# Low parts of eight weight pieces made by matrix products with plus and minus the identity instead of a VectorE subtraction

## Chip, core and metric

The kernel runs on one NeuronCore of one Trainium2 chip. The metric is the device time of one execution, in microseconds (us), lower is better. The core has TensorE (PE; its weight loads are listed apart as PEld), VectorE (DVE), ScalarE (ACT), GpSimd (POOL) and SyncE (SP, which here only issues transfers). Every engine has a queue of its own; they meet by semaphores.

## What is computed

A pooled attention, then a two-layer network with a leaky ReLU, then a mixture of eight experts with one expert for each token. Cut to what matters here:

```python
k_p = k.reshape(B, H, S // 8, 8, D).mean(axis=3)      # v_p likewise
attn = softmax(q @ k_p.T / sqrt(D))
x = attn @ v_p                                        # 4608 tokens x 512
h = x @ moe_w_in                                      # float64 weights, 512 x 2048
x = maximum(0.01 * h, h) @ moe_w_out                  # float64 weights, 2048 x 512
...
out[mask] = gate_w[mask, None] * (relu(x[mask] @ w1[e]) @ w2[e])
```

`moe_w_in` and `moe_w_out` come as 64-bit floating point numbers; all others as 32-bit.

## The kernel before

**Number format.** A product of the large stages is not done in fp32. Each operand is split into a high part (the value rounded to the type fp32r, in which TensorE streams a column in one pass) and a low part (value minus high part), and a product is the sum of three: high by high, high by low, low by high. So every weight tile holds both parts side by side. The low part is made with `sub`, a `tensor_tensor` subtraction (line 132, the line of the helper); the high part with `act_copy`, a copy on ACT (line 129).

**The dense network** runs over blocks of 256 tokens. A slot of the program is one pair (block b, piece f): `g1` (line 498) multiplies the block by the 128 columns of piece f of `moe_w_in` in twelve products, of which the third is the first to read a low part of the weights; ACT and DVE apply the leaky ReLU; two slots later `g2` (line 526) multiplies the result by piece f of `moe_w_out` in six products of 512 columns. There are sixteen pieces of either matrix. Slots 0 to 3 are pieces 0 to 3 of block 0; from slot 4 on, blocks 0 and 1 take turns.

**The weight pieces** are converted during the first slots. `w_load64` fetches a raw piece, 64-bit numbers, into one of seven raw tiles. `w_conv1` (lines 463 to 474) turns it into fp32 in place: ACT takes the absolute value of the top halfword (463) and prepares from it a word `e` (464) for the exponent; then DVE builds the fp32 word with four integer operations of 512 columns (465, 468, 471, 474), the first and last of which read `e`. The result lies in every second 32-bit word of the raw tile. `w_conv2` then writes the high part by ACT and the low part by DVE into the weight tile (tile `w00` and so on for `moe_w_in`, kind 0; `w10` and so on for `moe_w_out`, kind 1).

**The order of the work** is the order of the code: the program is emitted under a manual schedule, and each engine's queue follows it. A slot emits `g1`, the low part of an earlier activation (`g_lo`), the slot's hooks (attention steps for tokens still to come), the `g2` of two slots before, then `conv`, then the high part of the activation. In slots 0 to 3 `conv` does, for both kinds, first `w_conv2` of piece f+1 and then `w_conv1` of piece f+2. From slot 5 on it does one kind in a slot.

**The hooks of slots 0 to 3** are the attention steps of the third and fourth token tile: `att_a` and `att_b` of tile 2 in slot 0 and of tile 3 in slot 1 (transposes, then two groups of scores, which DVE reduces and subtracts from PSUM: lines 384 and 132), the softmax on ACT and DVE (390 to 399), `att_c` of tile 2 in slot 2 and of tile 3 in slot 3 (transposes, of which ACT takes a high and DVE a low part). In slot 4 `att_av` makes the activations of block 1. All of them take their PSUM bank with `pt("att")`, which hands out two banks in turn, `a0` and `a1`; a new user waits until the last user's readers are done.

Of the kernel before, what the change touches and what calls it, by code (L numbers as in the profile page):

```python
# [9 lines left out]
F32R = mybir.dt.float32r  # L10
# [11 lines left out]
def kernel(  # L22
# [12 lines left out]
    nc = tc.nc  # L35
    P = 128
# [3 lines left out]
    LAG = 4  # L40
# [8 lines left out]
    KD = DM // P  # L49
# [34 lines left out]
    def win(f):  # L84
        return wtile(0, f).rearrange("p (k h n) -> p k h n", k=KD, h=2)

    def wout(f):
        return wtile(1, f).rearrange("p (h n) -> p h n", h=2)
# [7 lines left out]
    ident = pool.tile([P, P], F32, name="ident")  # L96
# [15 lines left out]
    def sb(shape, dt, tag, bufs=1):  # L112
        return pool.tile(shape, dt, name=tag, tag=tag, bufs=bufs)
# [4 lines left out]
    def bank(tag):  # L118
        return psum.tile([P, 512], F32, name=tag, tag=tag)

    def pt(kind):
        turn[kind] += 1
        return bank(banks[kind][turn[kind] % len(banks[kind])])

    def f32(ap):
        return ap.bitcast(F32)

    def act_copy(o, i, scale=1.0):
        nc.scalar.activation(o, i, AF.Copy, scale=scale)  # L129

    def sub(eng, o, a, b):
        eng.tensor_tensor(out=o, in0=a, in1=b, op=ALU.subtract)  # L132
# [344 lines left out]
    def w_conv2(kind, f):  # L477
        w = f32(w_mid.pop((kind, f)))
        if kind == 0:
            w = w.rearrange("p (a n) -> p a n", a=KD)  # L480
            d = win(f)
            dh, dl = d[:, :, 0], d[:, :, 1]
        else:
            dh, dl = wout(f)[:, 0], wout(f)[:, 1]
        act_copy(dh, w)
        sub(nc.vector, dl, w, f32(dh))

    w_raw, w_mid, w_cnt = {}, {}, [0]

# [616 lines left out]
    with tc.manual_schedule():  # L1106
        stack = ExitStack()
        start = stack.enter_context(tc.tile_pool(name="start", bufs=1))
# [51 lines left out]
        att_c(1)  # L1160
        kv_use(0, 6)
        w_conv2(0, 0)
        w_conv1(1, 0)
        att_av(0)
        w_conv2(1, 0)
        kvn_load(0, k, 1)
        w_load64()
# [19 lines left out]
        def conv(s, b, f):  # L1187
            f += LAG * b
            kinds = (b,) if s > LAG and f < NF else (0, 1) if b == 0 else ()
            for kind in kinds:  # L1190
                if (kind, f + 1) in w_mid:
                    w_conv2(kind, f + 1)
                    if w_todo:
                        w_load64()
            for kind in kinds:
                if (kind, f + 2) in w_raw:
                    w_conv1(kind, f + 2)
# [171 lines left out]
```

## Time and profile before

| | |
|---|---|
| median of 3 runs | 1557.83 us (1556.98 to 1558.25) |
| the profiled execution | 1558.05 us, span 1556.0 us |
| granted TensorE clock, mean | 0.975 |
| PE matmul busy | 1472.8 us (95%) |
| PE weight load busy | 1317.6 us (85%) |
| DVE busy | 939.4 us (60%) |
| ACT busy | 626.8 us (40%) |
| POOL busy | 327.3 us (21%) |

The profile is of one execution. Times in it count from the start of the span. A granted clock of 1.00 is 2.4 GHz, of 0.50 1.2 GHz; a value between them in a window means that the clock changed inside it. A row of the timeline gives start, duration, engine, line, operation, output <- inputs, shapes and count, and in brackets the idle time before it and what ended it. Rows of one operation overlap a little at their ends, so the distance from start to start is what an operation costs its engine. An fp32 product appears as two MATMUL instructions, an fp32r product as one. Shares of busy time are averages over stages with different limits. In the trace, slot 0 starts at 35.5 us, and `g1` of slots 1 to 4 end near 49, 59, 69 and 76 us.

### The profile page before, as it was taken

The page shows a single profiled execution, that of the slowest core. Times are in us where ns is not written, and L with a number is a line of the kernel's source. Part 1 is how long each engine was busy: PE and PEld are TensorE (multiplying, and loading weights), DVE is VectorE, ACT ScalarE, POOL GpSimd, SP SyncE. Part 2 cuts the span into 40 slices and gives each one's busy share as a digit, 9 for nine tenths or more (in the row PEclk, how much of TensorE's full clock was granted, in tenths as well). Part 3 has the DMA queues.
Part 4 walks back from the last instruction along what each step waited for, and adds up shares of the span by engine and source line. Part 5 has one row for each costly group of instructions (what it writes and reads, how often), then busy time and mean ns, then how long its engine had stood idle before and what let it go on. Part 6 is the DMA issues. An engine that isn't in the chain of part 4 may idle for free. (4 is left out here: it accounts for less than half of the span.)

```text
span 1556.0 us, 25769 instructions
## 1 busy us (share of the span) xinstructions
PE 1472.8 (95%) x9272; PEld 1317.6 (85%) x9272; DVE 939.4 (60%) x2468; ACT 626.8 (40%) x1442; POOL 327.3 (21%) x294
## 2 busy tenths in 40 slices
PE   3698989999999999999999999999799999999998
PEld 3586879999898888899989989988699999998887
DVE  6998658879778878877877977664122121211111
ACT  4676434544444454444444444322122222222222
POOL 4000012232232233222222332121212111111111
PEclk8699999999999999999999999999899999999999
DMA  9443135555544545535645644143511117566160
GB/s 216 148 132 100 63 99 190 167 188 169 169 167 166 182 149 185 184 140 171 197 153 157 203 149 163 48 178 122 245 41 55 35 48 300 211 257 259 41 250 24
DMA packets 121386, 238.06 MB, mean 153 GB/s; under 512 B 56845, under 2 KB 65041, under 8 KB 117544
## 3 DMA queue, kind: packets, MB, share of 16 engines
q1 hardware_dynamic: 90312, 139.81, 28.7%
q10 hardware_dynamic: 23328, 76.56, 13.0%
q0 software_dynamic: 7616, 20.01, 3.8%
q8 instruction: 75, 1.23, 0.3%
q14 instruction: 55, 0.45, 0.1%
HBM read 317.78 MB, written 87.38 MB: 260 GB/s over the span
## 5 line engine op out<-in xcount | busy, mean ns | idle before, releaser
L526 PE MATMUL y<-w,ghl 128*128 128x512 f32 x1728 | 466.3, 406 | 2.8 <-DVE ghl L132 2.5
L526 PEld LDWEIGHTS y<-w,ghl 128*128 128x128 f32 x1728 | 310.1, 192 | 61.7 <-DVE ghl L132 6.3
L132 POOL TENSOR_TENSOR ps<-ps 128x512 f32<-128x512 f32 x128 | 181.6, 1419 | 482.2 <-ACT ps L129 361.8
L498 PEld LDWEIGHTS h<-x_t,w 128*128 128x128 f32 x1776 | 239.6, 195 | 39.8 <-DVE w L132 16.9
L498 PE MATMUL h<-x_t,w 128*128 128x256 f32 x1776 | 246.4, 288 | 24.0 <-DVE w L132 15.3
L546 DVE CUSTOM_DVE_ANT_0 junk<-y,wg 128x512 bf16<-128x512 f32 x256 | 200.3, 783 | 1.9
L498 PEld LDWEIGHTS y<-x_t,w 128*128 128x128 f32 x1488 | 193.2, 189 | 9.6
L498 PE MATMUL y<-x_t,w 128*128 128x256 f32 x1488 | 196.1, 282 | 0.0
L935 PE MATMUL y<-w,ghl 128*128 128x512 f32 x672 | 176.5, 401 | 0.9 <-DVE ghl L923 0.9
L935 PEld LDWEIGHTS y<-w,ghl 128*128 128x128 f32 x672 | 120.4, 190 | 22.4 <-DVE ghl L923 1.3
L129 ACT ACTIVATE g<-h 128x256 f32<-128x256 f32 x164 | 63.0, 384 | 145.9 <-PE h L498 132.8
L991 POOL DMA_INDIRECT out_dram<-kv,sidx x40 | 40.1, 1003 | 382.5 <-ACT kv L990 199.3
L923 DVE SCALAR_TENSOR_TENSOR ghl<-h,ghl 128x256 fp32r<-128x256 f32 x56 | 23.8, 425 | 135.9 <-ACT ghl L922 135.9
L506 DVE TENSOR_TENSOR h<-g,h 128x256 f32<-128x256 f32 x132 | 56.0, 424 | 77.7 <-ACT g L129 77.2
L132 DVE TENSOR_TENSOR at_t<-a,at_t 128x512 fp32r<-128x512 f32 x62 | 42.7, 688 | 87.6 <-ACT at_t L129 87.2
L129 ACT ACTIVATE ghl<-h 128x256 fp32r<-128x256 f32 x132 | 50.7, 384 | 92.9 <-PE y L526 42.8
L129 ACT ACTIVATE ps<-ps 128x512 fp32r<-128x512 f32 x128 | 80.5, 629 | 17.8 <-DMA ps<-in_moe_w_dram 8.7
L129 ACT ACTIVATE ghl<-y 128x256 fp32r<-128x256 f32 x124 | 47.3, 382 | 95.2 <-DVE y L506 50.5
L132 DVE TENSOR_TENSOR x_t<-a,x_t 128x512 fp32r<-128x512 f32 x60 | 41.1, 688 | 51.7 <-ACT x_t L129 51.7
L129 ACT ACTIVATE g<-y 128x256 f32<-128x256 f32 x124 | 47.4, 382 | 60.9 <-PE y L498 53.4
L295 DVE TENSOR_TENSOR kv<-kv 72x512 f32<-72x512 f32 (+8 forms) x126 | 68.0, 540 | 3.2
L613 POOL DMA_INDIRECT lst<-ent,six x36 | 37.8, 1051 | 150.4 <-DVE six L612 115.1
(291 smaller groups left out, 2157.2 us busy)
## 6 DMA issues: line engine op xcount, KB each, us to landing
w<-wsp SPq DMA_DIRECT2D x108, 2048.0 KB
wsp<-ps ACTq DMA_DIRECT2D x128, 512.0 KB
ps<-in_moe_w_dram SPq DMA_DIRECT2D x128, 256.0 KB
y_d<-y ACTq DMA_DIRECT2D x18, 512.0 KB
q<-in_q_dram SPq DMA_DIRECT2D x28, 256.0 KB
kv<-in_k_dram SPq DMA_DIRECT2D x24, 288.0 KB
kv<-in_v_dram SPq DMA_DIRECT2D x24, 256.0 KB
ps<-in_moe_w_in_dram SPq DMA_DIRECT2D x8, 512.0 KB
```

Source lines behind the costliest of these rows:

```text
L129: nc.scalar.activation(o, i, AF.Copy, scale=scale)
L132: eng.tensor_tensor(out=o, in0=a, in1=b, op=ALU.subtract)
L295: eng.tensor_tensor(out=o, in0=t[:, :, 0:w], in1=t[:, :, w:2 * w], op=ALU.add)
L498: nc.tensor.matmul(p[:, 0:BLK], win(f)[:, kk, l], xv[:, kk, r], start=(n == 0), stop=(n == 3 * KD - 1))
L506: nc.vector.tensor_tensor(out=g, in0=t, in1=h, op=ALU.max)
L526: nc.tensor.matmul(y_ps[b, i], hl[:, l, i * P:i * P + P], wout(f)[:, r], start=(f == 0 and l + r == 0), stop=(last and l == 1),)
L546: nc.vector.tensor_tensor_reduce(out=jk, in0=y_sb[b][:, i], in1=wg_t[0][:, e], scale=1.0, scalar=0.0, op0=ALU.mult, op1=ALU.add, accum_out ...
L613: nc.gpsimd.indirect_dma_start(out=lst, out_offset=bass.IndirectOffsetOnAxis(ap=ix[:, 0:1], axis=0), in_=ent[:, i, :], in_offset=None, bou ...
L923: nc.vector.scalar_tensor_tensor(out=hl[:, 1], in0=b, scalar=0.0, in1=f32(hl[:, 0]), op0=ALU.max, op1=ALU.subtract)
L935: nc.tensor.matmul(o_ps[2 * p + i], hl[:, l, i * P:i * P + P], w[:, r], start=(f == 0 and l + r == 0), stop=(f == 7 and l == 1),)
L991: nc.gpsimd.indirect_dma_start(out=out, out_offset=bass.IndirectOffsetOnAxis(ap=sidx[:, t:t + 1], axis=0), in_=o, in_offset=None, bounds_c ...
```

## The change

For pieces 1 to 4 of both kinds (eight pieces, converted in slots 0 to 3) the low part is no longer a subtraction on DVE. TensorE multiplies the fp32 piece by the identity (an fp32 product of 512 columns) and adds to it, in the same PSUM bank, the high part multiplied by minus the identity (an fp32r product of 512 columns); ACT copies the sum from PSUM into the weight tile. The bank comes from `pt("att")`. Minus the identity is made once, by ACT, in the buffer named `q`, which the load of the fifth token tile takes over in slot 4.

```diff
         act_copy(dh, w)
-        sub(nc.vector, dl, w, f32(dh))
+        if 1 <= f <= LAG:
+            if not minus:
+                minus.append(sb([P, P], F32R, "q"))
+                act_copy(minus[0], ident, -1.0)
+            p = pt("att")
+            pv = p.rearrange("p (a n) -> p a n", a=KD) if kind == 0 else p
+            nc.tensor.matmul(pv, ident, w, start=True, stop=False)
+            nc.tensor.matmul(pv, minus[0], dh, start=False, stop=True)
+            act_copy(dl, pv)
+        else:
+            sub(nc.vector, dl, w, f32(dh))
+
+    minus = []
```

The lines of the changed kernel behind this place are higher by 12 (`g1` is at 510 there, `g2` at 538); the two new products are at 492 and 493.

In ACT's queue, slot 1 before (a0 and a1 are the PSUM banks, w00 and w10 the weight tiles, r64 and kv raw tiles, e0 and e1 the words that `w_conv1` prepares):

```order
L390 ACTIVATE pr_385<-pr_385 128x576
L129 ACTIVATE w02_118<-a0_441 128x512
L129 ACTIVATE w00_301<-r64_114 128x4x128
L129 ACTIVATE w10_332<-kv_115 128x512
L463 ACTIVATE junk_109<-kv_116 128x512
L464 ACTIVATE e0_107<-junk_109,ebias_105 128x512
L463 ACTIVATE junk_109<-ps_110 128x512
L464 ACTIVATE e1_108<-junk_109,ebias_105 128x512
```

and the same place with the change:

```order
L390 ACTIVATE pr_385<-pr_385 128x576
L129 ACTIVATE w02_118<-a0_449 128x512
L129 ACTIVATE w00_301<-r64_114 128x4x128
L129 ACTIVATE w00_301<-a1_466 128x4x128
L129 ACTIVATE w10_332<-kv_115 128x512
L129 ACTIVATE w10_332<-a0_472 128x512
L463 ACTIVATE junk_109<-kv_116 128x512
L464 ACTIVATE e0_107<-junk_109,ebias_105 128x512
L463 ACTIVATE junk_109<-ps_110 128x512
L464 ACTIVATE e1_108<-junk_109,ebias_105 128x512
```

Two copies out of PSUM stand between the high parts and the operations of lines 463 and 464.

In PE's queue, slot 1 with the change, from the slot's `g1` to the next one:

```order
L510 MATMUL h0_425<-x_t_67,w00_301 128x256 x12
L359 MATMUL a0_449<-ident_76,w12_117 128x128 x4
L378 MATMUL a1_455<-kT0_70,w02_118 128x144 x2
L378 MATMUL a0_460<-kT0_70,w02_118 128x144 x2
L492 MATMUL a1_466<-r64_114,ident_76 128x512
L493 MATMUL a1_466<-w00_301,q_398 128x512
L492 MATMUL a0_472<-kv_115,ident_76 128x512
L493 MATMUL a0_472<-w10_332,q_398 128x512
L510 MATMUL h1_491<-x_t_67,w00_301 128x256 x12
```

The four rows of lines 492 and 493 are new, between the scores of `att_b` and the next `g1`; they use the banks a1 and a0 that the two groups of scores used just before.

## Rows read from the trace of the kernel before

**Rows 1.** Windows: us, busy of PE, PEld, DVE, ACT, POOL, then clock, DMA

```profile
41.00:83.00 42.00, 26.23 (x124) 22.79 (x124) 40.60 (x80) 26.81 (x48) 0.00 (x0) 0.72 0.47 146
83.00:175.00 92.00, 81.90 (x472) 68.23 (x471) 84.00 (x164) 58.62 (x121) 0.69 (x3) 0.93 0.30 92
```

**Rows 2.** Waits, 36 to 90 us: us in total, times, longest

```profile
PE h L498 <- DVE w L132: 13.0, 4, 3.9
...
DVE e L465 <- ACT e L464: 0.3, 1, 0.3
```

**Rows 3.** Timeline of DVE, slot 1

```profile
54.92 0.46 DVE L132 TENSOR_TENSOR w<-a,w 128x288 f32<-128x288 f32 x1
...
55.78 0.46 DVE L132 TENSOR_TENSOR w<-a,w 128x288 f32<-128x288 f32 x1
56.15 0.68 DVE L132 TENSOR_TENSOR w<-r,w 128x512 fp32r<-128x512 f32 x1
56.75 0.68 DVE L132 TENSOR_TENSOR w<-kv,w 128x512 fp32r<-128x512 f32 x1
57.35 0.69 DVE L465 SCALAR_TENSOR_TENSOR e<-kv,e 128x512 uint32<-128x512 uint32 x1
...
59.87 0.68 DVE L465 SCALAR_TENSOR_TENSOR e<-ps,e 128x512 uint32<-128x512 uint32 x1
...
62.40 0.41 DVE L506 TENSOR_TENSOR g<-g,h 128x256 f32<-128x256 f32 x1
```

**Rows 4.** Timeline of PE: scores, `g2` at either clock, fp32 products of 512 columns

```profile
50.35 2.29 PE L378 MATMUL a<-kT,w 128*128 128x144 f32 x8 [0.69 <-ACT w L129]
52.26 0.80 PE L498 MATMUL h<-x_t,w 128*128 128x256 f32 x2
...
60.32 2.63 PE L526 MATMUL y<-w,ghl 128*128 128x512 f32 x6
62.84 0.51 PE L498 MATMUL h<-x_t,w 128*128 128x256 f32 x2
...
91.84 1.53 PE L526 MATMUL y<-w,ghl 128*128 128x512 f32 x6
...
116.62 3.65 PE L267 MATMUL a<-w,band 128*64 128x512 f32 x8
```

**Rows 5.** Timeline of ACT, slots 0 and 1

```profile
43.64 0.66 ACT L129 ACTIVATE w<-y 128x512 fp32r<-128x512 f32 x1 [1.82 <-DVE y L474]
44.20 0.64 ACT L463 ACTIVATE junk<-r 128x512 bf16<-128x512 bf16 x1
44.88 0.72 ACT L464 ACTIVATE e<-junk,ebias 128x512 uint32<-128x512 uint16 x1
...
49.70 0.60 ACT L129 ACTIVATE w<-a 128x512 f32<-128x512 f32 x1
50.19 0.68 ACT L129 ACTIVATE w<-r 128x512 fp32r<-128x512 f32 x1
```

**Rows 6.** Timeline of DVE, attention and subtractions of slots 2 and 3

```profile
63.06 0.69 DVE L132 TENSOR_TENSOR at_t<-a,at_t 128x512 fp32r<-128x512 f32 x1
...
66.20 0.68 DVE L132 TENSOR_TENSOR w<-kv,w 128x512 fp32r<-128x512 f32 x1
...
73.11 0.68 DVE L132 TENSOR_TENSOR at_t<-a,at_t 128x512 fp32r<-128x512 f32 x1
...
74.26 1.29 DVE L132 TENSOR_TENSOR w<-ps,w 128x512 fp32r<-128x512 f32 x2
```

**Rows 7.** Windows of one microsecond; the clock is third from the end

```profile
52.00:53.00 1.00, 1.00 (x5) 0.77 (x4) 1.00 (x3) 1.00 (x2) 0.00 (x0) 0.50 0.00 0
62.00:63.00 1.00, 1.00 (x4) 0.57 (x4) 1.00 (x3) 1.00 (x3) 0.00 (x0) 0.76 0.00 0
65.00:66.00 1.00, 0.00 (x0) 0.00 (x0) 0.92 (x3) 0.97 (x3) 0.00 (x0) 0.94 0.00 0
```

**Rows 8.** Waits of PE over the whole span

```profile
PE a L900 <- DMA ps<-y_d,gidx: 9.1, 2, 8.8
```

## The prediction

> **What bounds the kernel now.** I began with the page, whose slices show VectorE (DVE) nearly full and TensorE's clock low early in the span, and cut that stage out. Over 41 to 83 us, where the slots of the change lie, DVE is busy 40.60 of 42.00 us and TensorE (PE) 26.23 [rows 1]. The waits say who holds whom: PE waits 13.0 us, four times, for DVE's write of a weight tile, while DVE waits 0.3 us for ScalarE's (ACT) sign-and-exponent word `e` [rows 2]. So DVE sets the pace, and the four waits are where PE needs the low part of the next piece.
>
> The timeline of DVE gives its order in a slot [rows 3]: at 54.92 and 55.78 the two groups of scores of `att_b` are read out of PSUM, at 56.15 and 56.75 come the two subtractions that the change removes, at 57.35 and 59.87 the repair of the two next raw pieces begins, and at 62.40 the activation of the next `g1`. A subtraction holds DVE for 0.60 us, though its own row says 0.68, since the next starts before its end. A piece's repair holds it 2.52 us (57.35 to 59.87).
>
> Later the delay has nothing to vanish into: from 83 to 175 us DVE is busy 84.00 of 92 us and PE 81.90 [rows 1]. I take what the stage gains or loses to pass to the end one for one.
>
> **The change part by part.** *Removed:* eight subtractions, 8 x 0.60 = 4.80 us of DVE time in a stretch with no free DVE time. By themselves they would give -4.80 us.
>
> *Added on PE:* eight fp32 products of 512 columns and eight fp32r ones. No row before shows the first kind at the low clock. At the full clock four of 512 columns (eight instructions, at 116.62) take 3.65 us, so about 0.90 us each; at the low clock four of 144 columns (eight instructions) take 50.35 to 52.26, or 3.32 ns per column, so 1.70 us for 512 (an estimate from these rows). An fp32r product of 512 columns takes 0.42 us at the low clock (six in 60.32 to 62.84) and about 0.25 us at the full one (six in 1.53) [rows 4]. A pair is thus 2.12 us or 1.15 us.
>
> *Added on ACT:* eight copies out of PSUM of 0.60 us, and one small copy that makes minus the identity, which falls in idle time and which I cost at nothing. ACT has room in total. What counts is where the copies stand. In program order a slot gives ACT: high part, low part out of PSUM, for either piece, and only then the two operations that prepare `e` for the next piece's repair. Before, those two followed the high parts at once. ACT doesn't let an operation that is ready pass one that waits: at 43.64 a copy starts after 1.82 us of waiting for DVE, and the absolute value behind it, whose data come by a transfer and not from DVE, starts at 44.20, after it [rows 5]. So a wait is added on ACT, and queued behind it is the word for which DVE must wait.
>
> *The chain that replaces the subtractions.* The first product needs a PSUM bank of the pair that the slot's attention step has just used, so it starts when DVE has read that bank. From there, at the low clock: both pairs of products 4.24, hand-over 0.05, low part of the second piece 0.60, absolute value 0.68 (44.20 to 44.88), `e` 0.72, hand-over 0.05: 6.34 us until DVE may begin the next repair. At the full clock the second piece's high part is late instead, as it stands on ACT behind the first low part: first pair 1.15, hand-over 0.05, low part 0.49 (49.70 to 50.19), high part 0.68, hand-over 0.05, second fp32r product 0.25, hand-over 0.05, then 0.60 + 0.68 + 0.72 + 0.05 as above: 4.77 us [rows 4, 5].
>
> DVE covers part of it with what it still has to do after freeing the bank:
> - slot 1: the first group's subtraction starts at 54.92 and lasts 0.46, so the bank is free at 55.38 and the product may start at 55.43; DVE has nothing left from 56.15 on. Cover 0.72 us [rows 3]. Slot 0 has the same operations; I take the same.
> - slot 2: bank free at 63.06 + 0.69, softmax work until 66.20. Cover 2.40 us [rows 6].
> - slot 3: bank free at 73.11 + 0.68, DVE free at 74.26. Cover 0.42 us [rows 6].
>
> *Which clock.* TensorE's granted clock is 0.50 (1.2 GHz) at 52 to 53 us though PE is busy all of that microsecond, 0.76 at 62 to 63 after PE has worked for some six microseconds, and 0.94 at 65 to 66, falling, with PE idle there [rows 7]. In slots 1 to 3 PE will again stand idle for several microseconds ahead of the first product, as DVE first does 5.04 us of repair, so I take the low clock for their products, and the full one for slot 0, which follows the dense stretch of the prologue. New DVE waits: 4.77 - 0.72 = 4.05; 6.34 - 0.72 = 5.62; 6.34 - 2.40 = 3.94; 6.34 - 0.42 = 5.92. Sum 19.53, less the 4.80 removed: **+14.7 us**. All four at the full clock: 4.05 + 4.05 + 2.37 + 4.35 = 14.82, so +10.0. All at the low one: 21.10, so +16.3.
>
> The Trainium skill weighs in against my choice: TensorE: Matmul & The Clock Gate, section "What's actually happening", says that activity releases the throttle, and this change adds activity. By that rule alone the sum would be the +10.0; the trace's busy microsecond at 0.50 does not bear it out so early in a burst.
>
> *Edits at no cost.* A raw tile is now free for its reload when the product has read it; these reloads fill tiles used slots later. The load of `q` for the fifth token tile shares its buffer with minus the identity and waits in SP's queue for slot 3's last product; it is read a dozen slots later. If that cover were short, the next transposes of `q` would wait.
>
> *A price no row shows.* The fp32 product streams a word out of every eight bytes; all PE rows here stream adjacent words. ACT reads the same eight-byte step in 0.68 us where a copy out of PSUM takes 0.60 [rows 5], so I take no extra; the other end, half speed, adds 2 x 1.70 per slot, 13.6 us in all. A gain is excluded, as a wider step carries no less. The Trainium skill, SBUF — State Buffer, in its note on cachelines under "The DMA port swizzle", has fp32 reads free up to a step of four elements, so by it no extra; no run here shows that yet.
>
> **The rivals.**
> - *Faster: DVE's relief passes through.* If ACT had `e` ready before DVE is done with attention, the stage would shrink by 8 x 0.60, to 1558.05 - 4.80 = 1553.3 us. For it: DVE is the full engine. It decides at the point where the chain is shorter than the cover (0.42 to 2.40 us); the absolute value and `e` alone take 1.40 us, more than the cover in three of four slots. Chance 0.04.
> - *The full clock in all four slots:* +10.0, 1568.1 us. For it: more PE work per slot. Against: the idle time ahead of each burst. Chance 0.17.
> - *Products at half speed for the eight-byte step:* +14.7 + 13.6 = +28.3, 1586.4 us. Chance 0.07.
> - *The loss is swallowed later,* about 1558 us: it takes a point tied to something other than this chain. The one long PE wait for a transfer, 8.8 us of 9.1, is for rows gathered after the routing [rows 8], which is itself at the end of the chain. Chance 0.03.
> - Forecast (low clock in most slots, +11 to +18): 0.66. The last 0.03 is for losses of another kind.
>
> **How the numbers follow.** The profiled execution took 1558.05 us with a span of 1556.0, and the median of the runs is 0.22 lower. 1558.05 + 14.7 = 1572.8 us. The range 1566 to 1580 holds the forecast, the all-full case at 1568.1 with 2 us of margin, the all-low case at 1574.4, and a third to a half of the half-speed penalty. Out of it stay the full half-speed case, the relief and the swallowed loss, together 0.14 and a little. A measurement of this kernel tells some 0.2% (3 us) from no change. Slower: 0.66 + 0.17 + 0.07 + 0.03 = 0.93; faster 0.04; within 0.2% 0.03.
>
> **What would show it.** In the changed profile DVE should have four waits of 4 to 6 us, all ended by ACT's `e`, where it had 0.3 us; PE's four waits for a weight tile from DVE should be gone, replaced by waits of the first identity product for DVE's reading of the bank. The end of slot 3 should lie about 15 us later, and the stretches after it should be shifted copies. The fp32 products should take about 1.7 us at a clock of 0.50 and 0.9 at 1.00. I am wrong if DVE runs through these slots without idle time, if `e` is written ahead of the low parts, or if the stages behind the slots take back the shift.

## The result and the profile after

| | before | with the change |
|---|---|---|
| median | 1557.4 us (1555.7 to 1558.25, 4 runs) | 1573.8 us (1571.46 to 1578.23, 4 runs) |
| span of the profiled execution | 1556.0 us | 1570.2 us |

The ratio is 1.011 (95% interval 1.0084 to 1.0136): slower, by 16.4 us in the medians and by 14.2 us between the two profiled executions. The forecast was 1572.8.

The page of the changed kernel, busy time of each engine:

```profile
PE 1483.9 (95%) x9296; PEld 1321.2 (84%) x9296; DVE 933.8 (59%) x2460; ACT 630.1 (40%) x1451; POOL 327.4 (21%) x294
```

The totals moved in the directions that the change says: DVE 5.6 us less (the eight rows of 0.68 that are gone make 5.4), PE 11 more, ACT 3.3 more. None of them tells that the kernel got slower. The waits between 36 and 106 us do (columns: us in total, times, longest us):

```profile
ACT w L129 <- PE a L493: 26.3, 8, 7.6
DVE e L465 <- ACT e L464: 21.9, 5, 6.2
...
PE a L492 <- DVE at_t L132: 9.8, 2, 5.0
PE a L492 <- issue: 7.3, 2, 4.4
```

The 13.0 us in which PE waited for DVE's low parts [rows 2] are gone; DVE's 0.3 us of waiting for `e` has become 21.9, and PE waits ahead of the new products. In slots 2 and 3 the profile names DVE's reading of the attention's bank as what ended PE's wait. In slots 0 and 1 it names nothing ("issue"), but there too the first product starts when DVE has just read the bank, 0.10 and 0.09 us after the end of the subtraction (44.31 + 0.46 and 59.62 + 0.46):

```profile
44.31 0.46 DVE L132 TENSOR_TENSOR pr<-a,st 128x288 f32<-128x288 f32 x1
44.87 2.04 PE L492 MATMUL a<-ps,ident 128*128 128x512 f32 x2 [2.93 <-issue]
...
59.62 0.46 DVE L132 TENSOR_TENSOR w<-a,w 128x288 f32<-128x288 f32 x1
60.17 2.04 PE L492 MATMUL a<-r,ident 128*128 128x512 f32 x2 [4.35 <-issue]
```

A circle has closed: PE waits for DVE, ACT for PE, DVE for ACT. The timeline of DVE shows the wait in each slot (the bracket at the end):

```profile
51.45 0.69 DVE L465 SCALAR_TENSOR_TENSOR e<-r,e 128x512 uint32<-128x512 uint32 x1 [5.82 <-ACT e L464]
...
66.37 0.69 DVE L465 SCALAR_TENSOR_TENSOR e<-kv,e 128x512 uint32<-128x512 uint32 x1 [5.44 <-ACT e L464]
...
79.43 0.69 DVE L465 SCALAR_TENSOR_TENSOR e<-ps,e 128x512 uint32<-128x512 uint32 x1 [4.13 <-ACT e L464]
...
92.49 0.69 DVE L465 SCALAR_TENSOR_TENSOR e<-y,e 128x512 uint32<-128x512 uint32 x1 [6.22 <-ACT e L464]
...
105.64 0.41 DVE L518 TENSOR_TENSOR g<-g,h 128x256 f32<-128x256 f32 x1
```

They sum to 21.61 us. Less the 4.80 of the eight subtractions that is 16.8; the last row, the activation of slot 5, stands at 88.62 before, so it came 17.0 us later.

One turn of the circle, slot 3, can be read across three engines. On DVE the attention's bank is read out, and then nothing is left:

```profile
85.14 0.68 DVE L132 TENSOR_TENSOR at_t<-a,at_t 128x512 fp32r<-128x512 f32 x1
85.86 0.41 DVE L132 TENSOR_TENSOR rm_t<-a,rm_t 32x256 fp32r<-32x256 f32 x1
```

On PE the first product starts 0.06 us after the first of these has ended:

```profile
85.88 2.08 PE L492 MATMUL a<-ps,ident 128*128 128x512 f32 x2 [4.90 <-DVE at_t L132]
86.97 1.42 PE L493 MATMUL a<-w,q 128*128 128x512 f32 x1
88.18 1.91 PE L492 MATMUL a<-ps,ident 128*128 128x512 f32 x2
89.62 0.90 PE L493 MATMUL a<-w,q 128*128 128x512 f32 x1
90.31 1.96 PE L510 MATMUL h<-x_t,w 128*128 128x256 f32 x12
```

And on ACT the two operations that make `e` come behind the second low part:

```profile
90.55 0.60 ACT L129 ACTIVATE w<-a 128x512 fp32r<-128x512 f32 x1 [0.98 <-PE a L493]
91.05 0.66 ACT L463 ACTIVATE junk<-y 128x512 bf16<-128x512 bf16 x1
91.74 0.72 ACT L464 ACTIVATE e<-junk,ebias 128x512 uint32<-128x512 uint16 x1
```

From 85.88 to 92.49 is 6.61 us: the products 4.43 (85.88 to 90.31), the hand-over to ACT 0.24, the copy 0.50, the two operations for `e` with the hand-over to DVE 1.44. DVE had 0.4 us of its own work in that time.

### The profile page after: what moved, and what is told of

Read it like the earlier page. It is cut to its first block, busy times and chain, and to the rows that moved or that the text cites. A ratio compares the mean times of both kernels' runs of the same rounds, so it can differ in the third digit from the quotient of the medians.

```text
span 1570.2 us, 25824 instructions
## 1 busy us (share of the span) xinstructions
PE 1483.9 (95%) x9296; PEld 1321.2 (84%) x9296; DVE 933.8 (59%) x2460; ACT 630.1 (40%) x1451; POOL 327.4 (21%) x294
## 3 DMA queue, kind: packets, MB, share of 16 engines
q8 instruction: 75, 1.23, 0.3%
## 5 line engine op out<-in xcount | busy, mean ns | idle before, releaser
L510 PE MATMUL h<-x_t,w 128*128 128x256 f32 x1776 | 242.4, 286 | 10.1 <-DVE ghl L132 4.6
L132 DVE TENSOR_TENSOR ghl<-h,ghl 128x256 fp32r<-128x256 f32 x132 | 55.5, 421 | 23.2 <-ACT ghl L129 22.7
```

Of the source, the lines that this page charges most:

```text
L510: nc.tensor.matmul(p[:, 0:BLK], win(f)[:, kk, l], xv[:, kk, r], start=(n == 0), stop=(n == 3 * KD - 1))
```

## The experiments

The measure beside the time is the stage: the way from the activation of slot 0 to that of slot 5 on DVE, 45.10 us before (43.52 to 88.62) and 62.14 with the change (43.50 to 105.64), +17.0. Two profiles of one kernel (runs 1 and 8) differ by 1.2 us in it, so differences of about that size in the stage say nothing. Runs 3 to 7 were timed once each, while the kernel before varied from 1551.64 to 1563.85 us beside them; of these runs the stage and the waits are read rather than the time.

**1. `e` ahead of the low parts.** `w_conv2` makes the high part and hands the rest back as a function; `conv` calls it after `w_conv1`. Same products, same banks; the reloads of the raw tiles move behind the low parts with it.

```diff
             for kind in kinds:
                 if (kind, f + 1) in w_mid:
-                    w_conv2(kind, f + 1)
-                    if w_todo:
+                    w_conv2(kind, f + 1, low)
+                    if w_todo and not low:
                         w_load64()
             for kind in kinds:
                 if (kind, f + 2) in w_raw:
                     w_conv1(kind, f + 2)
+            for lo in low:
+                lo()
+                if w_todo:
+                    w_load64()
```

> The two ACT operations that prepare `e` for the next pieces are put ahead of the low-part copies in ACT's queue; products, banks and clock rules stay. Theory A (DVE waits because `e` is queued behind the low parts): DVE's waits for `e` (21.6 us in four slots of the changed kernel) fall under 1 us, the activation of slot 5 comes between 3 and 5 us earlier than in the kernel before (88.6 there, 105.6 with the change), and the kernel takes 1552 to 1556 us. Theory B (the products are too long for TensorE, whatever the order): the products and `g1` now end after DVE's repair, DVE waits 1.5 us or more in a slot for `g1`, and slot 5 stays 5 to 9 us later than before, 1563 us or more. Theory C (the wait for the attention's PSUM banks costs the time): DVE's waits change by no more than a third, 1568 us or more.

Median 1551.66 us, ratio 0.9979 (0.9958 to 1.0000). The waits of DVE between 36 and 104 us:

```profile
DVE e L465 <- ACT e L464: 2.4, 5, 0.9
DVE g L522 <- ACT g L129: 0.7, 2, 0.5
```

So 21.9 us of waiting fell to 2.4. Of these, 0.9 us (0.3 and 0.6) stand in the trace of the kernel before as well, and 0.3 belong to slot 4. In the four slots 21.6 us became 1.2 (0.36 in slot 2 and 0.87 in slot 3), a little more than the 1 us expected, since there ACT gets to `e` only after its own softmax and attention copies. The activation of slot 5 stands at 85.67, 3.0 us earlier than before (3 to 5 were expected); the stage takes 42.55 us, 2.5 less than before and 19.6 less than with the change, with every product still there. Theory A holds. B, which wanted 1563 us or more, falls, and so does C as a cause that works without the queue.

**2. The same, in banks of its own.** In addition:

```diff
-            p = pt("att")
+            p = bank(f"y{2 + kind}")
```

> As the first, and the products write two PSUM banks that nothing else uses in these slots (y2 and y3), so they needn't wait until DVE has read the attention's banks. Theory A: little left to gain, within 1.5 us of the first kernel (1551 to 1556 us), DVE without waits over 1 us. Theory B: 1560 us or more, as the work on TensorE is the same. Theory C: this, and not the first, brings the time back to 1558 us or less.

Median 1555.01 us, ratio 0.9997 (0.9974 to 1.0021); the stage takes 41.03 us, 4.1 less than before, and DVE waits 1.6 us for `e`, of which 0.3 in the four slots. That is 1.5 us better than the profile of the first run, but run 8, the same kernel as the first, has the same waits (1.6, and 0.3 in the four slots) and a stage of 41.39 us: banks of their own add nothing that shows once `e` goes first. In the timed runs nothing is gained over the kernel before that the interval shows. B falls again; C too, since the first run had brought the time back without it.

**3. TensorE kept busy ahead of the products.** The changed kernel with twelve products whose result nothing reads:

```diff
+            if s < LAG:
+                p = bank("y3")
+                for _ in range(12):
+                    nc.tensor.matmul(p, win(0)[:, 0, 0], wout(0)[:, 0], start=True, stop=True)
             if s < 2 * NF:
                 conv(s, b, f)
```

> The changed kernel with twelve fp32r products of 512 columns (about 3 us at the full clock), whose result nothing reads, ahead of the pieces' products in slots 0 to 3, so that TensorE stands idle for about 1.5 to 2 us there and not 3 to 5. Theory A with its term for the clock: the granted clock is 1.00 in the pieces' products, an fp32 product of 512 columns takes about 0.9 us where it took 1.1 and 1.4 in either half, DVE's waits for `e` are 4.0, 4.0, 2.4 and 4.3 us (15 in all, 21.6 before), and slot 5 comes 10 us later than in the kernel before, not 17. If the clock doesn't matter to the waits, they stay at 21 us. If the added products delay the pieces' products, the waits grow by 1 us or more in a slot.

1569.29 us in one run. In the windows of the two profiles (columns: window, its length, PE busy, granted clock, DMA share, GB/s) slot 0 is first that of the changed kernel,

```profile
43.00:44.00 1.00, 0.00 (x0) 0.67 1.11 333
44.00:45.00 1.00, 0.13 (x1) 0.50 0.99 378
45.00:46.00 1.00, 1.00 (x3) 0.50 1.08 370
```

where the clock falls to 0.50 while PE stands idle and stays there through the products; and with the added products

```profile
45.00:46.00 1.00, 1.00 (x4) 1.00 1.01 363
46.00:47.00 1.00, 1.00 (x3) 1.00 1.00 283
```

the full clock. A pair of products then takes 1.20 us (44.77 to 45.97) and not 2.27 (44.87 to 47.14). DVE's waits became 4.33, 4.33, 3.64 and 5.04, 17.3 us, as in slots 2 and 3 the clock fell all the same during the products (0.71 at 70 to 71 us, 0.54 at 84 to 85). The stage is 12.8 us longer than before, and not 17. So the clock is a part of the loss, 1.5 us in slot 0 (5.82 to 4.33) and 1.1 in slot 1 (5.44 to 4.33), and the smaller part. The rule of the Trainium skill that activity releases the throttle (TensorE: Matmul & The Clock Gate, "What's actually happening") agrees with slots 0 and 1 of this run. Slots 2 and 3 got as much added work, stood idle for 2.2 us behind it, and lost the clock during the products. With the change alone the products came after the idle time and ran at the low clock in all four slots, but for the last one of slot 1.

**4. Shorter products.** Both products fp32r, plus and minus the identity with the high part; the low parts of these eight pieces are left out:

```diff
-                minus.append(sb([P, P], F32R, "q"))
+                t = sb([P, 2, P], F32R, "q")
+                minus.extend([t[:, 0], t[:, 1]])
                 act_copy(minus[0], ident, -1.0)
+                act_copy(minus[1], ident)
...
-            nc.tensor.matmul(pv, ident, w, start=True, stop=False)
+            nc.tensor.matmul(pv, minus[1], dh, start=True, stop=False)
```

> The changed kernel with the fp32 product replaced by an fp32r product of the identity with the high part, so that the low part of these eight pieces comes out as zero (it leaves out the low part of eight weight pieces); same count of waits, banks and copies, less TensorE work. Theory A: the queue on ACT still holds `e` back, by 4.2, 4.2, 2.6 and 4.5 us at the low clock or 3.6, 3.6, 1.9 and 3.9 at the full one: 13 to 15.5 us of DVE waits in all, slot 5 8 to 11 us later than in the kernel before. Theory B: without the long products the waits fall under 6 us in all and slot 5 comes no later than before.

1569.05 us in one run; the stage is 13.6 us longer than before. DVE's four waits are 4.92, 4.93, 3.25 and 5.08 us, 18.2 in all. That refutes B, which wanted under 6, and is 2.7 us more than A's upper figure, since a pair with its hand-over to ACT costs more than I had it (below): in slot 0 it takes 1.23 and 1.26 us (44.68 to 45.91 and 47.11 to 48.37), where two products of 0.42 and a hand-over of 0.05 make 0.89. The shorter products save less than they are shorter by, because the second pair now waits for the second piece's high part on ACT, which with the change had been made while the products ran:

```profile
47.11 0.79 PE L494 MATMUL a<-w,q 128*128 128x512 f32 x1 [1.24 <-ACT w L129]
```

The profile puts the first of these waits down to a transfer, but ACT's `e` ends at 50.27 (49.55 + 0.72) and DVE starts at 50.31:

```profile
50.31 0.69 DVE L465 SCALAR_TENSOR_TENSOR e<-r,e 128x512 uint32<-128x512 uint32 x1 [4.92 <-DMA y<-in_moe_w_in_dram]
```

**5. Own banks alone.** The changed kernel with the edit of run 2 and ACT's order as changed.

> The changed kernel, ACT's order as changed (`e` behind the low parts), but the products write the unused PSUM banks y2 and y3 and so start as soon as TensorE is free and the raw pieces are repaired, about 2 to 5 us earlier in a slot. Theory A: `e` is still behind the low parts, but these are done while DVE still works on attention, so only the slots in which DVE has little left after its repair (0 and 3) keep a wait, 1 to 3 us each; waits of DVE for `e` 2 to 6 us in all (21.9 in the changed kernel), slot 5 between 3 us earlier and 2 us later than in the kernel before. If the banks play no part, waits stay above 18 us.

1559.03 us in one run, waits of DVE for `e` 5.8 us, the stage 45.29 us, as before. With the banks free the products start while DVE is still at work (the first at 42.34 and not 44.87), and three slots keep 1.4 to 1.7 us of wait: 0 and 3, as expected, and 1. So there are two ways to open the circle: take `e` out of the queue behind the products, or start the products earlier. Run 1 shows that the first is enough; this one, that the bank is where the chain begins.

**6 and 7. One slot alone.** Products for piece 3 only, and for piece 4 only:

```diff
-        if 1 <= f <= LAG:
+        if f == 3:
```

(and `f == 4`).

> Only the two pieces converted in slot 2 (number 3 of either kind) get their low part by products, the six others by subtraction. Theory A with cover: one wait of DVE for `e` of 3.9 to 4.2 us, less two subtractions (1.2), so slot 5 comes 2.7 to 3.0 us later than in the kernel before. If DVE's softmax work in that slot gave no cover, it would be 6 us and 4.8.

> Only the two pieces converted in slot 3 (number 4 of either kind) get their low part by products. Theory A with cover: one wait of DVE for `e` of 5.9 to 6.3 us at the low clock (4.3 at the full one), less 1.2, so slot 5 comes 4.7 to 5.1 us later than in the kernel before (3.1 at the full clock). If the waits of the four slots only appear together, 1 us or less.

1560.27 and 1560.52 us, one run each. DVE's wait in slot 2 of the one and slot 3 of the other:

```profile
68.99 0.69 DVE L465 SCALAR_TENSOR_TENSOR e<-ps,e 128x512 uint32<-128x512 uint32 x1 [2.64 <-ACT e L464]
```

```profile
78.74 0.69 DVE L465 SCALAR_TENSOR_TENSOR e<-y,e 128x512 uint32<-128x512 uint32 x1 [4.73 <-ACT e L464]
```

Each stands alone, so the waits don't need each other, and the difference of 2.09 is what DVE's softmax work covers in slot 2 (reckoned: 2.40 - 0.42 = 1.98). Both are 1.49 us shorter than the same waits in the changed kernel (4.13 and 6.22): here PE had been idle for only 1.55 and 0.64 us and the products ran at the full clock (1.00 from 63 and from 73 us on). That measures the clock's share a second time. The stage got 1.6 and 3.5 us longer, against 2.64 - 1.20 and 4.73 - 1.20 (1.4 and 3.5). For slot 2 I had expected 2.7 to 3.0, at the low clock.

**8. The first run once more, five rounds.**

> The kernel of the first run once more, with more rounds, to settle whether it beats the kernel before: in its profile the stage gains 3 us. Theory A: ratio 0.996 to 0.999. If the gain of the stage is lost in later stages: 1.000 or more.

Median 1553.57 us against 1556.81, ratio 0.9970 (0.9956 to 0.9984). It beats the kernel before by 0.3%, a little more than the 0.2% that can be told, and the change by more than 1%. Its stage takes 41.39 us, 3.7 less than before, of which 3.2 arrive in the medians.

## Why the prediction was right, and where a step was off

- *The mechanism.* DVE's four waits came where they were foretold: at line 465, for `e` from ACT, behind the low parts, 4.1 to 6.2 us each. Run 1 takes them away by moving ACT's order (and, with it, the reloads). That is shown. The end of slot 3 lies 17.0 us later, where about 15 was forecast.
- *Products, price.* Pairs of 2.12 us at the low clock and 1.15 at the full one were reckoned; measured are 2.27 to 2.30 for a slot's first pair and 2.13 to 2.14 for the second (slots 0, 2 and 3), and 1.20 to 1.24 at the full clock (runs 3, 6 and 7). The forecast of 1.7 us for an fp32 product by itself can't be read: the next product starts 1.06 to 1.44 us after it, and its row lasts 1.72 to 2.08. A slot's two pairs took 4.41 to 4.44 us in these three slots, where products at half speed would have made 7.64 (4.24 + 3.40), so that rival falls. The note on cachelines of the Trainium skill (SBUF — State Buffer, "The DMA port swizzle") has fp32 reads free up to a step of four elements; these rows, with a step of two, agree.
- *The clock of slot 0 was the step that failed.* "The full one for slot 0, which follows the dense stretch of the prologue": the clock fell at 43 to 44 us, in the 2.9 us in which PE waited ahead of the first product, and the wait was 5.82 us, not 4.05. The trace of the kernel before already had this fall, in the idle time of the same slot (columns as in run 3):

```profile
44.00:45.00 1.00, 0.00 (x0) 1.00 1.01 385
45.00:46.00 1.00, 0.00 (x0) 0.70 1.07 363
46.00:47.00 1.00, 0.70 (x3) 0.50 0.45 136
```

  The other three were taken at the low clock rightly (in slot 1 it rose at 63 to 64 us, before the last product), and the rival of a full clock in all slots falls with them. The waits measured at the full clock (4.33 and 4.33 in run 3, 2.64 in run 6, 4.73 in run 7) sum to 16.0 us, so by these three executions the low clock is some 5.6 of the 21.6 us.
- *The hand-over was mis-sized by 0.2 us.* Each wait is 0.2 to 0.4 longer than reckoned at its clock where the clock held (4.13 for 3.94, 6.22 for 5.92; 2.64 for 2.37 and 4.73 for 4.35 in runs 6 and 7). I took a product as the distance to the next start. That is what it costs PE, but not when ACT may read: in slot 3 the last product's row ends at 90.52 (89.62 + 0.90, an end that the profile models), its successor had started at 90.31, and ACT starts at 90.55, 0.24 after that and not 0.05. The products were another 0.2 us longer than reckoned (4.43 for 4.24) and the copy 0.1 shorter (0.50 for 0.60).
- *"One for one to the end" held for most of it.* The shift of the activations is 17.0 us at slot 5 and 17.35 at 152 us of the kernel before, then 16.06, 15.26 and, at 1051 us, 14.05. Row against row, before:

```profile
152.47 0.41 DVE L506 TENSOR_TENSOR g<-g,h 128x256 f32<-128x256 f32 x1
...
178.31 0.42 DVE L506 TENSOR_TENSOR g<-g,h 128x256 f32<-128x256 f32 x1 [2.05 <-ACT g L129]
...
246.46 0.42 DVE L506 TENSOR_TENSOR h<-g,h 128x256 f32<-128x256 f32 x1
...
1051.53 0.43 DVE L506 TENSOR_TENSOR h<-g,h 128x256 f32<-128x256 f32 x1 [1.24 <-ACT g L129]
```

  and with the change:

```profile
169.82 0.42 DVE L518 TENSOR_TENSOR g<-g,h 128x256 f32<-128x256 f32 x1
...
194.37 0.42 DVE L518 TENSOR_TENSOR g<-g,h 128x256 f32<-128x256 f32 x1 [1.22 <-ACT g L129]
...
261.72 0.42 DVE L518 TENSOR_TENSOR h<-g,h 128x256 f32<-128x256 f32 x1
...
1065.58 0.43 DVE L518 TENSOR_TENSOR h<-g,h 128x256 f32<-128x256 f32 x1 [1.21 <-ACT g L129]
```

  Ahead of the row at 178.31 the kernel before waits 2.05 us for PE, and the changed kernel, at 194.37, only 1.22: the conversion has ended, DVE now waits for PE, and PE had lost time in one execution that it had not in the other. Of two `g1`, the same in either kernel, the first took 2.76 us before and 1.60 with the change (1.2 of the first 1.3 us that the shift lost), the second, after 3.95 us of waiting in either, 2.93 and 2.33 (0.6 of the next 0.8 us). Before:

```profile
165.65 2.76 PE L498 MATMUL h<-x_t,w 128*128 128x256 f32 x12
...
221.05 2.93 PE L498 MATMUL h<-x_t,w 128*128 128x256 f32 x12 [3.95 <-DVE ghl L132]
```

  and with the change:

```profile
182.67 1.60 PE L510 MATMUL h<-x_t,w 128*128 128x256 f32 x12
...
237.13 2.33 PE L510 MATMUL h<-x_t,w 128*128 128x256 f32 x12 [3.96 <-DVE ghl L132]
```

  For the first of them the granted clock was 0.50 before (165 to 168 us) and 1.00 with the change (182 to 185). What makes the clock fall at another place in one execution than in the other stays open, as do the last steps of the shift, up and down by 1.5 us.
- *Luck in the number.* The forecast of 1572.8 rests on two errors of opposite sign: 21.6 us of waits for 19.5, and 2.8 us given back later where none was reckoned. Of the second, 1.8 us lie in two products that met the low clock in one execution and not, or for less long, in the other, so they belong to this pair of executions and not to the change. The medians, 16.4 us apart, show less of it.

## What to carry to other kernels

Before moving work off the full engine, write down each queue in order: an engine with plenty of idle time can still hold up the full one, if a short operation that the full engine needs stands behind one that now waits for somebody else. Put first in a queue what the bound engine waits for, and take scratch banks from a pool that the bound engine does not release. Busy totals would have promised a gain of 4.8 us here; the same products give 2.5 to 3.7 us in the stage (runs 1 and 8) once ACT prepares `e` ahead of the low parts.

## What the runs showed of the hardware

With the change the first pair of a slot's products took 2.27 to 2.30 us after PE had stood idle for 2.9 to 5.0 us, with a granted clock of 0.50 as it began. The same pair took 1.20 to 1.24 us in runs 3, 6 and 7 after 0 to 1.6 us of idle time, at 1.00. The length of the idle time does not settle it by itself: in run 3 the pairs after 2.2 us took 2.04 us (slot 2) and 1.24 (slot 3), and in run 8 the first pair took 2.27 us after 1.32 us, as the clock had stood at 0.50 from before 40 us on.

I had not expected that shorter products (run 4) would leave more than four fifths of the wait, 18.2 of 21.6 us. In the changed kernel the products are 4.43 of the 6.61 us of slot 3's turn. In run 4 the turn of slot 0 still takes 5.63 us (44.68 to 50.31): 2.49 for two shorter pairs with their hand-overs, and the rest for copies, a high part and `e`.
